# Moving read-outs and tanh behind the next exponentials, and turning the row maxima on VectorE

## The chip, the core and the metric

The kernel runs on one NeuronCore of a Trainium2 chip. Five engines work side by side, each through its own queue in order: TensorE (PE) multiplies matrices into PSUM banks, VectorE (DVE) and ScalarE (ACT) read those banks, GpSimd (POOL) works on SBUF only, and SyncE (SP) issues the transfers. PSUM has eight banks of 128 partitions by 512 fp32 values. The metric is the device time of one execution in microseconds; lower is better.

## The reference

One transformer layer with attention and MLP in parallel, all in fp32, with S = 2048 tokens, D = 512, H = 32 heads of 16, and F = 1792:

```
xn  = layernorm(x)
q, k, v = split(xn @ wqkv)                       # 32 heads of 16
p   = softmax(q k^T / 4)                         # per head, 2048 x 2048
out = x + (p v) @ wo + gelu_tanh(xn @ w1 + b1) @ w2 + b2
```

## The kernel before

**Precision.** Most fp32 matrices are split into a high and a low fp16 part and multiplied by three products (high·high, high·low, low·high). p·v is done in fp32.

**Attention.** Heads are taken in 8 groups of four (NG), query tokens in four blocks of 512 (NQB), keys in 16 blocks of 128. A pair (group, query block) is called t; there are 32. One *unit* u is a sixteenth of a t, so there are 512 units, and each unit has two *halves* (a = 0, 1). The softmax needs the maximum of each query row before the exponentials, so there are two passes over the scores, both on PE, the second one 19 units (LEAD) behind the first:

- `s_half` (L245): scores with queries on the partitions, into a bank of the list S; VectorE reduces the tile to row maxima, tile `mt` (L257). 4 tiles a unit.
- `s_end` (L260): at the last unit of a t, `mneg` takes the maximum over the key blocks (L268). The maxima must then lie along the free dimension, as two extra rows (high and low fp16 part) of the query operand `qst`, rows 62 and 63 of each half of 64, where a row of constants in `kst` subtracts them inside the product. A function `store` is left in a dictionary and called in the first half of the next unit (L674). It transposes `mneg` with two fp32 products against the identity into a bank of S (L275), VectorE splits it to `mhl` (L278, L279), two transfers write `m_d` in memory (L282) and four read it back into `qst` (L287).
- `e_half` (L291): scores with keys on the partitions, into a bank of the list T; ScalarE takes exp into `pe` (L302). 4 tiles a unit; the first that needs the maxima of t is in unit 16t + 19.
- `v_half` (L305): p·v, accumulated over a whole t in the bank of the list V. At the end ScalarE copies it to `osb` (L328), and VectorE, POOL and transfers divide it by the row sums.

**Dense work.** All other products (projections of q and k, MLP, output projection) are cut into *groups* that fill one bank: 12 products for a hidden tile (56 of them, 14 per block of 512 tokens), 42 for an output tile (16). PE is used as two halves of 64 rows: in each half-unit one side does p·v and the other side `dense` (L575) adds three or four products of the current group (`pace`), each cut in four tiles of 32 columns by `tiled` (L195; the products themselves are issued on L169). When a group is complete, `ended` calls `end` (L444), which emits the read-out on ScalarE and returns the group's bank. The read-outs are: `hh` (L1045, hidden tiles), `yt` (L1068, MLP output tiles), `pf` (L502, projections of q and k), `ys` (L1109, output projection).

**gelu.** After `hh`, POOL makes three steps (L1025 to L1027), ScalarE the tanh on tile `t1` (L1014, shown as `t`), POOL four more steps (L1019 to L1022) that end in the two fp16 parts `g`. These steps are put off by units: `later(n, fn)` runs fn n units later at the unit's end (`tick`, L233), and `pooled` gives POOL about 2.5 us of steps a unit.

**Order.** From unit 16 on the order is written out by hand: `unit` (L633) emits, for each half, two score tiles and two exponential tiles (the *burst*: S, E, S, E), then p·v and dense products, then what is due. Each engine keeps that order. The projections of the first key group run before, in a set-up stage ordered by a planner.

**Banks.** `free_banks` (L102) holds lists. S has three banks; the bank for p·v comes from V the first time and then from S, to which it returns. T has three; the group's bank comes from D the first time, and from the front of T afterwards, since `hold("D", "T")` gives a bank that returns to the end of T. So four banks serve the exponential tiles and the group: while a group holds one, three rotate; in the moment between two groups, T holds four. `banks` takes from the front of the list and puts it back at the end at once: waiting for the earlier reader is left to the hardware semaphores.

```
def end(self):
    self.finish(self.bank)
    if self.key is not None:
        free_banks[self.key[1]].append(self.key[0])
```

Of the kernel before, what the change touches and what calls it, by code (L numbers as in the profile page):

```python
# [8 lines left out]
F32 = mybir.dt.float32  # L9
F16 = mybir.dt.float16  # L10
I32 = mybir.dt.int32
AF = mybir.ActivationFunctionType
ALU = mybir.AluOpType
AX = mybir.AxisListType
# [3 lines left out]
P = 128  # L18
S = 2048
# [8 lines left out]
NQB = S // QB  # L28
NG = H // 4
# [13 lines left out]
MROW = 1024.0  # L43
# [4 lines left out]
def layer_kernel(ctx: ExitStack, tc: tile.TileContext, x, wqkv, wo, w1, b1, w2, b2, out):  # L48
    nc = tc.nc
    x = x.flatten_outer_dims()  # L50
    out = out.flatten_outer_dims()

    def pool(stack, name, bufs=1, space=None, side=None):
        kw = {k: v for k, v in (("space", space), ("side", side)) if v is not None}
        return stack.enter_context(tc.tile_pool(name=name, bufs=bufs, **kw))

    const = pool(ctx, "const")
    work = pool(ctx, "work")
    ps = pool(ctx, "ps", space=PSUM)
    dram = pool(ctx, "dram", space=DRAM)  # L60
# [4 lines left out]
    w1_d = dram.tile([NF // 2, P, 2, 2, NC, P], F16, name="w1_d")  # L65
    w2_d = dram.tile([P, 2, NF, D], F16, name="w2_d")
    acc_d = dram.tile([S, D], F32, name="acc_d")
    m_d = dram.tile([NG * NQB, 16, 2, P], F16, name="m_d")
    ot_d = dram.tile([D, 2, S], F16, name="ot_d")
    den_d = dram.tile([NG * NQB, 2, 4, QB], F32, name="den_d")  # L70

# [1 line left out]
    ident = const.tile([P, P], F32, name="ident")  # L73
# [19 lines left out]
    nc.gpsimd.memset(vv[:, :, H * VW:], 0.0)  # L93
    wo_s = const.tile([P, 2, NC, D], F16, name="wo_s")
    sexp = const.tile([P, 4], F32, name="sexp")

    mnegs = [const.tile([P, 32], F32, name=f"mneg{i}") for i in range(2)]
    for m in mnegs:
        nc.gpsimd.memset(m, 0.0)


    free_banks = {"S": [0, 1, 2], "T": [3, 4, 5], "D": [6], "V": [7]}  # L102
# [1 line left out]
    def bank_tile(k, tag):  # L104
        return ps.tile([P, QB], F32, tag=f"B{k}", bufs=1, name="p" + tag)

    def banks(tag):
        k = free_banks[tag].pop(0)
        free_banks[tag].append(k)
        return bank_tile(k, tag)  # L110
# [48 lines left out]
    def given(engine, ns):  # L159
        backlog[engine] += ns  # L160
# [26 lines left out]
    def enter():  # L187

        if left:
            goal[0] = f"turn{counted[0]}"  # L190
            for p in left:
                tc.add_to_no_dep_group(goal[0], p.ins)
            left.clear()
# [9 lines left out]
    def fetch_scale(m):  # L203

        scale_of[m] = nc.scalar.alloc_register(f"sexp{m}")
        nc.scalar.reg_load(scale_of[m], sexp[0:1, m:m + 1].bitcast(I32))

    mt_of, ptiles, pv_of, stores = {}, {}, {}, {}
    queue, slot = [], [0]

    def later(n, fn, local=False):
        queue.append((slot[0] + n, fn, local))

    def run_due():
        due = sorted((q for q in queue if q[0] <= slot[0]), key=lambda q: q[0])
        queue[:] = [q for q in queue if q[0] > slot[0]]
        for q in due:
            q[1]()


    steps, room = [], [0]
# [4 lines left out]
    def run_steps(all_of_them=False):  # L226
        room[0] = min(room[0], 0) + POOL_NS
        while steps and (room[0] > 0 or all_of_them):
            ns, fn = steps.pop(0)
            room[0] -= ns  # L230
            fn()
# [5 lines left out]

    def flush():

        while steps or any(q[2] for q in queue):  # L240
            run_due()
            run_steps(True)
            slot[0] += 1

# [15 lines left out]
    def s_end(u):  # L260

        t, i = divmod(u, 16)
        if i < 15:
            return
        g, qb = divmod(t, NQB)
        qs = qst[g % 2]
        mneg = mnegs[t % 2]
        nc.vector.tensor_reduce(mneg[:, :16], mt_of[t].rearrange("p h t k -> p (h t) k"), axis=AX.X, op=ALU.max, negate=True)  # L268
        given("dve", 220)

        def store():

            pt = banks("S")
            for a in range(2):
                nc.tensor.matmul(pt[32 * a:32 * a + 32, :64], mneg[64 * a:64 * a + 64, :],  # L275
                                 ident[64 * a:64 * a + 64, 64 * a:64 * a + 64], start=True, stop=True)
            mhl = work.tile([64, 2, 64], F16, name="mhl", bufs=2)
            nc.vector.tensor_scalar_mul(mhl[:, 0], pt[:64, :64], 1.0 / MROW)  # L278
            nc.vector.scalar_tensor_tensor(mhl[:, 1], pt[:64, :64], 1.0 / MROW, mhl[:, 0], op0=ALU.mult, op1=ALU.subtract)  # L279
            given("dve", 300)  # L280
            for a in range(2):
                nc.sync.dma_start(m_d[t, :, :, 64 * a:64 * a + 64], mhl[32 * a:32 * a + 16])  # L282
            for p in range(2):
                for a in range(2):
                    h = 2 * p + a
                    dst = qs[p][qb][64 * a + 62:64 * a + 64, :].rearrange("r (t q) -> r t q", q=P)
                    nc.sync.dma_start(dst, m_d[t, 4 * h:4 * h + 4].rearrange("t r q -> r t q"))  # L287

        stores[t] = store

    def e_half(u, n):  # L291

# [264 lines left out]
                cur[0], spent[0] = None, True  # L557
        return cur[0]

    def ended():  # L560

        if cur[0] is not None and cur[0].over():
            done, cur[0] = cur[0], None
            done.end()

    def burst(gen, n):

# [49 lines left out]

    def land():

        while extra[0] is not None:  # L620
            for side in range(2):
                if extra[0] is not None:
                    spare(None, side)
        if cur[0] is not None:
            enter()
        for side in range(2):
            while cur[0] is not None and cur[0].left(side):
                nc.tensor.drain()
                while cur[0].left(side):
                    cur[0].product(side)  # L630
        ended()

    def unit(gen):  # L633


        u = pos[0]
        e = u - LEAD
        if e >= 0 and e % (2 * NQB * 16) == 0 and e < NU:
            fetch_scale(e // (2 * NQB * 16))
        if u == LEAD and cur[0] is not None:  # L640
            burst(gen, cur[0].left())
        pos[0] += 1
        for a in range(2):
            for b in range(2 * a, 2 * a + 2):
                if u < NU:
                    s_half(u, b)
                elif u > NU:
                    spare(gen, b % 2)
                if 0 <= e < NU:
                    e_half(e, b ^ 1)  # L650
            if u < LEAD:
                burst(gen, LFILL[u - 16] // 2)
            if e >= 0:
                enter()

                w, r = (e - 2, 1) if a == 0 else (e - 1, 0)
                live = 0 <= w < NU
                new = r == 0 and w % 16 == 0
                if live and not new:
                    v_half(w, r)  # L660
                dense(gen, 1 - r)
                if live and new:
                    v_half(w, r)

                for user, goes_on in (("V", live and not (r == 1 and w % 16 == 15)),
                                      ("D", cur[0] is not None and not cur[0].over())):
                    leave(user, goes_on)
                for k in backlog:
                    backlog[k] = max(0, backlog[k] - HALF)
                if live and r == 1:  # L670
                    v_end(w)
                ended()

            if a == 0 and u % 16 == 0 and u // 16 - 1 in stores:  # L674
                stores.pop(u // 16 - 1)()
        if u < NU:
            s_end(u)
        tick()
# [325 lines left out]
    def mlp():  # L1004
# [3 lines left out]
        done = set()  # L1008

        def gelu(hh, g, b, f):  # L1010
            t1 = m2.tile([P, QB], F32, name="t1", bufs=2)

            def tanh():
                nc.scalar.activation(t1, t1, AF.Tanh, scale=GELU_C * GELU_A)  # L1014
                given("act", 600)
                later(1, rest, True)

            def rest():
                pooled((690, lambda: nc.gpsimd.tensor_scalar(t1, t1, 1.0, gs[:, 1:2], op0=ALU.add, op1=ALU.mult)),  # L1019
                       (1280, lambda: nc.gpsimd.tensor_tensor(t1, t1, hh, op=ALU.mult)),  # L1020
                       (620, lambda: nc.gpsimd.tensor_scalar(g[:, 0, f, :], t1, 1.0, 0.0, op0=ALU.mult, op1=ALU.add)),
                       (1160, lambda: nc.gpsimd.tensor_tensor(g[:, 1, f, :], t1, g[:, 0, f, :], op=ALU.subtract)),  # L1022
                       (0, lambda: done.add((b, f))))

            pooled((1040, lambda: nc.gpsimd.tensor_tensor(t1, hh, hh, op=ALU.mult)),  # L1025
                   (620, lambda: nc.gpsimd.tensor_scalar(t1, t1, 1.0, 1.0 / GELU_A, op0=ALU.mult, op1=ALU.add)),
                   (1280, lambda: nc.gpsimd.tensor_tensor(t1, t1, hh, op=ALU.mult)),  # L1027
                   (0, lambda: later(2, tanh, True)))

        for b in range(NQB):  # L1030
            xb = xbs[b]
# [19 lines left out]
            for q in range(4):  # L1051
                t = b * 4 + q
# [13 lines left out]
                def store(yp, xa=xa, t=t):  # L1066
# [9 lines left out]
                            lambda n, b=b: (b, n // 3) in done, pace=SLOW if b < 2 else MEAN)  # L1076
# [151 lines left out]
```

## Time and profile before

| | |
|---|---|
| runs shown | 1526.5, 1520.38 and 1525.09 us, median 1525.09 |
| profiled execution | 1520.55 us, its span 1518.8 us |
| busy share of the span | PE 98%, VectorE 92%, ScalarE 82%, POOL 44% |
| granted clock of PE | 0.996 on average |
| score reductions (L257) | 2048, 1304.5 us busy together |
| exponentials (L302) | 2048, 1100.8 us busy together |

The page is one execution: its first part gives the busy time of each engine, its second the span in 40 slices, its fourth the chain of work that ended last, its fifth the costliest groups of instructions with the idle time ahead of them and what ended it. Two matrix products on different row halves or column tiles overlap, so a busy PE does not say how much of it works. A row of the timeline gives start, length, engine, line, output and input, and in brackets the idle time before it and who ended that.

The score passes start at about 38 us; the hand-written order runs from about 107 us to the end. Projections of q and k fill the dense side until about 304 us, then come hidden stage and output stage for each of the four blocks (to 1385 us), then the output projection.

### The profile page before, as it was taken

Reading aid. Unit: us, or ns where it says so; the run is one execution under the profiler, and the core shown is the slowest. Engines: PE = TensorE matmul, PEld = TensorE weight load, DVE = VectorE, ACT = ScalarE, POOL = GpSimd, SP = SyncE. Lnnn points to the kernel's source line nnn. Section 1 sums busy time; section 2 is a strip of 40 time slices with the busy share of each in tenths; the row PEclk is TensorE's granted clock in tenths of the full one; section 3 lists DMA queues with packets and bytes.
Section 4 is the critical chain, followed back from the end, with each engine's and each line's share of the span. In section 5 each row is a group of like instructions: output and inputs, shape, how many; then the busy total and the mean of one; then the engine's idle time right before and its main releaser. Section 6 shows DMA issues by size and latency. Waiting matters only on the chain.

```text
span 1518.8 us, 86848 instructions
## 1 busy us (share of the span) xinstructions
PE 1489.5 (98%) x39407; PEld 815.9 (54%) x39407; DVE 1402.2 (92%) x2367; ACT 1245.6 (82%) x2318; POOL 664.5 (44%) x686
## 2 busy tenths in 40 slices
PE   8999999999999999999999999999999999999998
PEld 3434555555555555555555555555555555555553
DVE  7899989999999999999999999999999999999933
ACT  5327778899988888898888898988888898888884
POOL 4113597547771112777411167751116775211110
PEclk9999999999999999999999999999999999999998
DMA  6454567542122201121011211122101201121422
GB/s 208 127 155 158 166 219 211 180 126 77 58 69 66 61 26 42 36 84 50 23 49 41 66 42 40 36 78 63 34 25 56 77 27 29 50 60 50 136 65 95
DMA packets 113674, 123.76 MB, mean 81 GB/s; under 512 B 24988, under 2 KB 85276, under 8 KB 113304
## 3 DMA queue, kind: packets, MB, share of 16 engines
q1 hardware_dynamic: 113304, 118.21, 25.4%
q8 instruction: 308, 5.05, 1.4%
q14 instruction: 62, 0.51, 0.1%
HBM read 80.61 MB, written 37.34 MB: 78 GB/s over the span
## 4 chain that ended last, share of the span: by engine, by line
PE 79%; DVE 16%; issue 2%; ACT 2%; DMA 1%; POOL 0%; SPq 0%; POOLq 0%
PE pV L169 23%; PE pD L169 19%; PE pT L169 17%; PE pS L169 16%; DVE mt L257 13%; PE pT L435 1%; PE pD L435 1%; DVE amx L709 1%; ACT pe L302 1%; ACT t L1014 1%; PE pT L528 1%; PE pV L528 0%; DMA m_d<-mhl 0%; DMA xs<-in_A_x_dram 0%; DMA wch<-in_B_w_dram 0%
## 5 line engine op out<-in xcount | busy, mean ns | idle before, releaser
L257 DVE TENSOR_REDUCE mt<-pS 128x1 f32<-128x512 f32 x2048 | 1304.5, 684 | 52.5 <-PE pS L169 34.8
L302 ACT ACTIVATE pe<-pT 128x512 f32<-128x512 f32 x2048 | 1100.8, 599 | 162.9 <-PE pS L169 78.6
L169 PE MATMUL pV<-pe,vv 64*32 64x512 f32 x8192 | 1076.3, 595 | 0.1
L169 PE MATMUL pT<-qst,kst 64*32 64x512 f16 x8192 | 718.3, 378 | 8.8 <-ACT pe L302 7.9
L169 PE MATMUL pS<-kst,qst 62*32 62x512 f16 x8192 | 624.3, 378 | 5.2 <-DVE mt L257 3.6
L169 PEld LDWEIGHTS <-kst 64*32 64x32 f16 x8192 | 285.7, 91 | 203.9 <-issue 103.6
L169 PEld LDWEIGHTS <-qst 62*32 62x32 f16 x8192 | 273.3, 92 | 206.3 <-issue 58.2
L169 PE MATMUL pD<-w_s,g 64*32 64x512 f16 x5376 | 364.6, 376 | 0.0
L169 PE MATMUL pD<-xb,wc 64*32 64x512 f16 x5376 | 360.9, 377 | 0.0
L169 PEld LDWEIGHTS pV<-pe,vv 64*32 64x32 f32 x8192 | 181.0, 105 | 88.3 <-PE pV L169 4.3
L1070 POOL TENSOR_TENSOR xa<-xa,yt 128x512 f32<-128x512 f32 x16 | 20.5, 1282 | 319.0 <-ACT yt L1068 319.0
L169 PEld LDWEIGHTS <-wc 64*32 64x32 f16 x5376 | 116.9, 91 | 41.6
L169 PEld LDWEIGHTS <-g 64*32 64x32 f16 x5376 | 112.2, 91 | 45.3
L169 PE MATMUL pD<-xt,wqk_h 64*32 64x512 f16 x2016 | 134.7, 377 | 1.7 <-issue 1.5
L1025 POOL TENSOR_TENSOR t<-hh 128x512 f32<-128x512 f32 x56 | 58.3, 1041 | 132.7 <-ACT hh L1045 121.8
L358 POOL TENSOR_TENSOR osb<-osb,rb 128x512 f32<-128x512 f32 x31 | 39.9, 1287 | 135.1 <-DMA rb<-den_d 76.0
L1027 POOL TENSOR_TENSOR t<-t,hh 128x512 f32<-128x512 f32 x56 | 71.9, 1284 | 4.7
L1020 POOL TENSOR_TENSOR t<-t,hh 128x512 f32<-128x512 f32 x56 | 71.8, 1281 | 4.7
L1022 POOL TENSOR_TENSOR g<-t,g 128x512 f16<-128x512 f32 x56 | 65.2, 1165 | 4.7
L169 PEld LDWEIGHTS <-wqk_h 64*32 64x32 f16 x2016 | 47.5, 92 | 23.4 <-issue 6.2
L169 PE MATMUL pD<-wo_s,oc 64*32 64x512 f16 x828 | 54.5, 378 | 0.0
L1045 ACT ACTIVATE hh<-pD,b_s,fac 128x512 f32<-128x512 f32 x56 | 43.6, 779 | 9.4 <-PE pT L169 3.3
(141 smaller groups left out, 862.4 us busy)
## 6 DMA issues: line engine op xcount, KB each, us to landing
wch<-in_B_w_dram SPq DMA_DIRECT2D x28, 512.0 KB
wc<-w_d SPq DMA_DIRECT2D x56, 256.0 KB
qk_d<-stg SPq DMA_DIRECT2D x32, 256.0 KB
rb<-den_d SPq DMA_DIRECT2D x124, 64.0 KB
w_d<-wsp SPq DMA_DIRECT2D x28, 256.0 KB
kst<-qk_d SPq DMA_DIRECT2D x128, 48.0 KB
qst<-qk_d SPq DMA_DIRECT2D x128, 48.0 KB
xs<-in_A_x_dram SPq DMA_DIRECT2D x16, 256.0 KB
```

The costliest lines, as they stand in the source:

```text
L169: p = nc.tensor.matmul(*args, **kw)
L257: nc.vector.reduce_max(mt_of[t][:, n, qt, kb:kb + 1], s, axis=AX.X)
L302: nc.scalar.activation(pe, st, AF.Exp, scale=scale_of[g // 2])
L358: pooled((1280, lambda: nc.gpsimd.tensor_tensor(osb, osb, rb, op=ALU.mult)), (620, lambda: nc.gpsimd.tensor_scalar(ot[:, 0], osb, 1.0, 0.0 ...
L435: nc.tensor.matmul(self.bank, lhs, rhs, start=start, stop=self.last and self.over())
L528: nc.tensor.matmul(pj, xt[:, i, c, t * P:(t + 1) * P], wh[j][:, c, :], start=(n == 0), stop=(n == 11))
L1020: (1280, lambda: nc.gpsimd.tensor_tensor(t1, t1, hh, op=ALU.mult)),
L1022: (1160, lambda: nc.gpsimd.tensor_tensor(g[:, 1, f, :], t1, g[:, 0, f, :], op=ALU.subtract)),
L1025: pooled((1040, lambda: nc.gpsimd.tensor_tensor(t1, hh, hh, op=ALU.mult)), (620, lambda: nc.gpsimd.tensor_scalar(t1, t1, 1.0, 1.0 / GELU_A ...
L1027: (1280, lambda: nc.gpsimd.tensor_tensor(t1, t1, hh, op=ALU.mult)),
L1045: nc.scalar.activation(hh, hp, AF.Identity, scale=scale, bias=bias)
L1070: add = lambda: nc.gpsimd.tensor_tensor(xa, xa, yt, op=ALU.add)
```

## The change

Two things are moved and one is replaced.

- **Read-outs.** `ended` can now leave the group's `end` in a list `ends`; `unit` calls `ended(False)`, and `one_more()` takes one entry in the next half, after that half's burst and before its p·v and dense products. So the read-out stands on ScalarE behind the two exponentials of the next burst instead of ahead of them, and the bank returns to T after that burst has drawn its two banks. The next group still starts in the same half as before.
- **tanh.** When it is due, it goes to a list `extras`, of which `one_more` takes one entry when no read-out is waiting. So it too stands behind a burst's exponentials, and never directly next to a read-out.
- **Maxima.** `s_end` no longer leaves a function for the next unit. VectorE splits `mneg` into high and low part side by side (`mh`, 128 x 32 fp16) and turns it with its 32x32 transposition into `mc`, in which partition 32b + c holds column c of the 32 queries of block b. Four transfers write that to `m_d` (32 rows of 64 bytes each, before two of 128-byte runs), and four read it back in rows of 1024 bytes (before 256). The two products on PE, their bank of S, the two constant tiles `mnegs` and their clearing are gone. All this is emitted at the end of the last unit of t, half a unit and a burst earlier than before.

```
-    m_d = dram.tile([NG * NQB, 16, 2, P], F16, name="m_d")
+    m_d = dram.tile([NG * NQB, 2, 16, P], F16, name="m_d")
...
     def flush():
-        while steps or any(q[2] for q in queue):
+        settle()
+        while steps or extras or any(q[2] for q in queue):
             run_due()
+            while extras:
+                extras.pop(0)()
             run_steps(True)
...
-        mneg = mnegs[t % 2]
-        nc.vector.tensor_reduce(mneg[:, :16], mt_of[t].rearrange("p h t k -> p (h t) k"), axis=AX.X, op=ALU.max, negate=True)
+        mneg = work.tile([P, 16], F32, name="mneg", bufs=2)
+        nc.vector.tensor_reduce(mneg, mt_of[t].rearrange("p h t k -> p (h t) k"), axis=AX.X, op=ALU.max, negate=True)
         given("dve", 220)

-        def store():
+        mh, mc = (work.tile([P, 32], F16, name=x, bufs=2) for x in ("mh", "mc"))
+        nc.vector.tensor_scalar_mul(mh[:, :16], mneg, 1.0 / MROW)
+        nc.vector.scalar_tensor_tensor(mh[:, 16:], mneg, 1.0 / MROW, mh[:, :16], op0=ALU.mult, op1=ALU.subtract)
+        nc.vector.transpose(mc, mh)
+        rows = m_d[t].rearrange("j c q -> (j c) q")
+        for b in range(4):
+            nc.sync.dma_start(rows[:, 32 * b:32 * b + 32], mc[32 * b:32 * b + 32])
+        for p in range(2):
             for a in range(2):
-                nc.tensor.matmul(pt[32 * a:32 * a + 32, :64], mneg[64 * a:64 * a + 64, :],
-                                 ident[64 * a:64 * a + 64, 64 * a:64 * a + 64], start=True, stop=True)
...
+                h = 2 * p + a
+                nc.sync.dma_start(qs[p][qb][64 * a + 62:64 * a + 64, :],
+                                  m_d[t, :, 4 * h:4 * h + 4].rearrange("j t q -> j (t q)"))
...
+    ends, extras = [], []
+
+    def ended(at_once=True):
         if cur[0] is not None and cur[0].over():
             done, cur[0] = cur[0], None
-            done.end()
+            ends.append(done.end)
+            if at_once:
+                settle()
+
+    def settle():
+        while ends:
+            ends.pop(0)()
+
+    def one_more():
+        if ends:
+            ends.pop(0)()
+        elif extras:
+            extras.pop(0)()
...
             if e >= 0:
+                one_more()
                 enter()
...
-                ended()
-
-            if a == 0 and u % 16 == 0 and u // 16 - 1 in stores:
-                stores.pop(u // 16 - 1)()
+                ended(False)
...
-                   (0, lambda: later(2, tanh, True)))
+                   (0, lambda: later(2, lambda: extras.append(tanh), True)))
```

More of the change, by code (lines that the diff above doesn't have):

```diff
@@ L95, in layer_kernel @@
     sexp = const.tile([P, 4], F32, name="sexp")
-    mnegs = [const.tile([P, 32], F32, name=f"mneg{i}") for i in range(2)]
-    for m in mnegs:
-        nc.gpsimd.memset(m, 0.0)
     free_banks = {"S": [0, 1, 2], "T": [3, 4, 5], "D": [6], "V": [7]}
@@ L206, in fetch_scale @@
         nc.scalar.reg_load(scale_of[m], sexp[0:1, m:m + 1].bitcast(I32))
-    mt_of, ptiles, pv_of, stores = {}, {}, {}, {}
+    mt_of, ptiles, pv_of = {}, {}, {}
     queue, slot = [], [0]
@@ L266, in s_end @@
         qs = qst[g % 2]
-        mneg = mnegs[t % 2]
-        nc.vector.tensor_reduce(mneg[:, :16], mt_of[t].rearrange("p h t k -> p (h t) k"), axis=AX.X, op=ALU.max, negate=True)
+        mneg = work.tile([P, 16], F32, name="mneg", bufs=2)
+        nc.vector.tensor_reduce(mneg, mt_of[t].rearrange("p h t k -> p (h t) k"), axis=AX.X, op=ALU.max, negate=True)
         given("dve", 220)
-        def store():
-            pt = banks("S")
-            for a in range(2):
-                nc.tensor.matmul(pt[32 * a:32 * a + 32, :64], mneg[64 * a:64 * a + 64, :],
-                                 ident[64 * a:64 * a + 64, 64 * a:64 * a + 64], start=True, stop=True)
[L277 to L289, printed above, removed]
+        mh, mc = (work.tile([P, 32], F16, name=x, bufs=2) for x in ("mh", "mc"))
[6 more added lines that the diff above has]
+        for p in range(2):
+            for a in range(2):
+                h = 2 * p + a
+                nc.sync.dma_start(qs[p][qb][64 * a + 62:64 * a + 64, :],
+                                  m_d[t, :, 4 * h:4 * h + 4].rearrange("j t q -> j (t q)"))
     def e_half(u, n):
@@ L558, in group @@
         return cur[0]
-    def ended():
+    ends, extras = [], []
+    def ended(at_once=True):
         if cur[0] is not None and cur[0].over():
             done, cur[0] = cur[0], None
-            done.end()
+            ends.append(done.end)
[9 more added lines that the diff above has]
+            extras.pop(0)()
     def burst(gen, n):
@@ L618, in land @@
     def land():
+        settle()
         while extra[0] is not None:
```

## The prediction

> **What bounds the kernel now.** I read the page first, for the engines' shares and the chain that ended last; then the busy table by stage, restricted to the score reductions of line 257; then the order in time around single events.
>
> ```profile
> span 1518.8 us, 86848 instructions
> PE 1489.5 (98%) x39407; PEld 815.9 (54%) x39407; DVE 1402.2 (92%) x2367; ACT 1245.6 (82%) x2318; POOL 664.5 (44%) x686
> ...
> DMA  6454567542122201121011211122101201121422
> ...
> PE 79%; DVE 16%; issue 2%; ACT 2%; DMA 1%; POOL 0%; SPq 0%; POOLq 0%
> ```
>
> The DMA line is its busy share in 40 slices, in tenths. PE carries four fifths of the chain, VectorE most of the rest, ScalarE 2%. A unit is four reductions and four exponentials, so the count of reductions in a window, divided by four, gives the pace. The eight windows below are in turn the hidden-layer stage and the output stage of each of the four token blocks; columns: window, length, VectorE busy (instructions), clock, DMA share, GB/s.
>
> ```profile
> 306.20:440.00 133.80, 125.01 (x197) 1.00 0.28 84
> 440.00:585.50 145.50, 141.48 (x225) 1.00 0.17 48
> 585.50:719.50 134.00, 125.13 (x197) 1.00 0.20 59
> 719.50:865.40 145.90, 141.74 (x225) 1.00 0.14 42
> 865.40:998.60 133.20, 125.07 (x197) 1.00 0.15 45
> 998.60:1124.90 126.30, 122.67 (x192) 1.00 0.17 49
> 1124.90:1258.80 133.90, 125.03 (x197) 1.00 0.18 53
> 1258.80:1385.20 126.40, 122.55 (x193) 1.00 0.14 40
> ```
>
> One edge reduction aside, a hidden window is 49 units: 534.9 us over 196, 2.729 us a unit. The last two output windows are 48 units each and carry the same dense load (3.5 products a half on average): 252.7 us over 96, 2.632. So the hidden stages pay 0.097 us a unit, 19.0 us in all, for what the output stages have less of: read-outs of 56 groups and 56 tanh. Where that goes is seen in time, ScalarE first and then PE:
>
> ```profile
> 929.74 2.28 ACT L302 ACTIVATE pe<-pT 128x512 f32<-128x512 f32 x4 [0.28 <-PE pS L169]
> 932.15 0.78 ACT L1045 ACTIVATE hh<-pD,b_s,fac 128x512 f32<-128x512 f32 x1
> 932.83 0.62 ACT L1014 ACTIVATE t<-t 128x512 f32<-128x512 f32 x1
> 933.35 2.05 ACT L302 ACTIVATE pe<-pT 128x512 f32<-128x512 f32 x4
> 933.99 0.40 PE L169 MATMUL pT<-qst,kst 64*32 64x512 f16 x4 [0.39 <-ACT pe L302]
> ```
>
> The read-out and the tanh stand ahead of the next burst's exponentials; these begin at 933.35, 1.1 us late, and the score product that wants their bank begins at 933.99. A lone read-out costs less, as in an output stage:
>
> ```profile
> 826.47 2.27 ACT L302 ACTIVATE pe<-pT 128x512 f32<-128x512 f32 x4 [0.28 <-PE pS L169]
> 828.82 0.69 ACT L1068 ACTIVATE yt<-pD,gs 128x512 f32<-128x512 f32 x1
> 829.40 2.05 ACT L302 ACTIVATE pe<-pT 128x512 f32<-128x512 f32 x4
> 831.69 2.29 ACT L302 ACTIVATE pe<-pT 128x512 f32<-128x512 f32 x4 [0.24 <-PE pS L169]
> ```
>
> Two units from 826.47 to 831.69 are 5.22 us. An undisturbed unit is 2.55 (847.03 to 849.58 below), so the yt cost 0.12.
>
> **The change, part 1: read-outs and tanh behind the exponentials.** The order of PE's products stays; only ScalarE's order and the PSUM banks change. It gives back the 19.0 us of the hidden stages and the price of the other read-outs:
>
> ```profile
> L1045 ACT ACTIVATE hh<-pD,b_s,fac 128x512 f32<-128x512 f32 x56 | 43.6, 779 | 9.4 <-PE pT L169 3.3 <-PE pS L169 2.8
> L502 ACT ACTIVATE pf<-pD 128x512 f32<-128x512 f32 x22 | 13.1, 597 | 7.4 <-PE pD L435 2.9 <-PE pS L169 2.3 <-PE pT L169 2.2
> L1068 ACT ACTIVATE yt<-pD,gs 128x512 f32<-128x512 f32 x16 | 11.0, 688 | 1.5 <-PE pT L169 0.2
> L1109 ACT ACTIVATE ys<-pD,gs 128x512 f32<-128x512 f32 x8 | 5.5, 687 | 1.0 <-PE pT L169 0.6
> ```
>
> That is 22 + 16 + 8 = 46 others; at 0.12 for yt and somewhat less for the shorter pf I take 0.10, 4.6 us. The gain if nothing takes their place: 23.6 us.
>
> Something does. The group's bank used to return to the rotation at the end of its half, before the next burst drew its two banks; now it returns after they are drawn. Follow the list of free T banks. Before, it held four at that moment, and every score tile got a bank whose last exponential was three tiles back. After, it holds three; the burst takes z and x, the read-out returns k behind them, the new group takes y from the front, and the second burst again gets z and x: two tiles back. k comes only in the third. So in each of these 102 places the second score tile of a burst waits for the second exponential of the burst just before. Undisturbed, these stand so:
>
> ```profile
> 847.03 2.28 ACT L302 ACTIVATE pe<-pT 128x512 f32<-128x512 f32 x4 [0.28 <-PE pS L169]
> 847.52 0.59 ACT L302 ACTIVATE pe<-pT 128x512 f32<-128x512 f32 x1
> 847.75 0.57 PE L169 MATMUL pT<-qst,kst 64*32 64x512 f16 x5
> 849.58 1.79 ACT L302 ACTIVATE pe<-pT 128x512 f32<-128x512 f32 x3 [0.28 <-PE pS L169]
> ```
>
> The second exponential ends at 848.11. The last product of the next burst's second tile is the one that ends at 848.32; a product takes 0.38, so it starts at 847.94. It would have to wait until 848.11 plus the signal's way (at 933.99 the product came about 0.05 after the exponential that began at 933.35 and takes 0.59): 0.22 us. V stands behind it in PE's queue, so the wait is paid in full where PE is full; with four dense products a half the tile comes a little later anyway. Between 0 and 0.22 I take 0.20: 102 x 0.20 = 20.4 us lost. Net of part 1: -3.2 us.
>
> The Trainium skill, Perfetto Trace Analysis, Optimization Strategy, says that the same gap repeating for a stretch on the engine that should be saturated can mean too little PSUM for the next tile. By that rule the kernel still lacks a bank, and moving the read-out only moves the gap; the row at 933.99 agrees, since there PE waits for a bank.
>
> The later hh and tanh (one to one and a half units each) I cost at nothing. PE's dense products stand in the same halves in both built programs, and an output group takes the hidden tiles in order, three products each, so the last of 14 is wanted after 39 products at three or four a unit: about ten units, 26 us, after the stage's end. POOL's seven steps and the tanh are 7 us by the costs in the code, plus some four units of waiting slots, now five or six. If that cover went, PE would wait for POOL at four places, once a block.
>
> **Part 2: the maxima.** VectorE and the one PE wait at such a boundary, before:
>
> ```profile
> 809.84 0.68 DVE L257 TENSOR_REDUCE mt<-pS 128x1 f32<-128x512 f32 x1
> 810.55 0.22 DVE L268 TENSOR_REDUCE mneg<-mt 128x16 f32<-128x64 f32 x1
> 810.69 1.28 DVE L257 TENSOR_REDUCE mt<-pS 128x1 f32<-128x512 f32 x2
> 811.89 0.21 DVE L278 TENSOR_SCALAR mhl<-pS 64x64 f16<-64x64 f32 x1
> 812.13 0.22 DVE L279 SCALAR_TENSOR_TENSOR mhl<-pS,mhl 64x64 f16<-64x64 f32 x1
> 812.02 0.40 PE L169 MATMUL pS<-kst,qst 62*32 62x512 f16 x4 [0.16 <-DVE mt L257]
> ```
>
> Removed: the PE products of line 275 and the S bank they drew, and the two mhl instructions between reductions. Added: three in a row behind mneg (split high, split low, transposition). Nearest rows:
>
> ```profile
> L758 DVE SCALAR_TENSOR_TENSOR sd<-sd 128x4 f32<-128x4 f32 x4 | 0.6, 158 | 0.1
> L346 DVE RECIPROCAL dn<-dn 64x32 f32<-64x32 f32 x31 | 10.4, 334 | 0.0
> ```
>
> I take 0.17 for each split (16 columns, where the row has four) and, with no row for a transposition, 0.20, nearer the first row (bounds 0.16 from it and 0.33 from the second, 32 columns and a slow operation). With 0.03 between dependent instructions (809.84 + 0.68 to 810.55) the stretch from 810.52 is 0.9, less 0.08 by which a reduction overlaps its predecessor: 0.82. The next reduction then ends at 810.52 + 0.82 + 0.68 = 812.02, and the second score tile of that half, which now needs this reduction's bank (the S rotation is one shorter), comes at 812.07 against 812.02 today. Today's came after the later reduction because line 275 had drawn a bank. So one wait replaces the other at about equal price; VectorE, left 0.2 further behind, makes PE wait about 0.1 once more. I take +0.10 for 29 boundaries under full load, +2.9 us (bounds -5 and +9).
>
> The Trainium skill, VectorE: DVE Perf Modes, Rules for kernel authors, advises fewer operations in a chain, not cheaper links; the same page's The three transpose paths gives 311 ns for 128x128. At 0.31 for the transposition part 2 would cost an estimated 6 us.
>
> The way through memory grows from six transfers to eight:
>
> ```profile
> 812.37 1.22 SPq L282 DMA_DIRECT2D m_d<-mhl  x2
> 814.82 1.16 SPq L287 DMA_DIRECT2D qst<-m_d  x4
> 818.05 0.39 PE L169 MATMUL pT<-qst,kst 64*32 64x512 f16 x4
> ```
>
> Four stores at 0.61 from 811.4 end at 813.8; with the same 1.23 between them and the loads, and 0.29 a load, the last is issued by 816.2, against 815.98 now, and the first product that reads them stands at 818.05. In SP's queue the stores now stand ahead of the transfers of the unit's end instead of behind them; these wait for the transposition too and follow the loads. They are fetches for later units. I count 0.
>
> **Sum.** -3.2 + 2.9 + 0 = -0.3 us on the profiled execution's 1520.55 (span 1518.8), which is 4.5 below the median of the runs shown, 1525.09. On the median: about 1524, no change.
>
> **The rivals.** (A) The two-tile reuse is absorbed, because exponentials ahead of read-outs run earlier than in my undisturbed unit. For it: the margin is 0.2 us and PE starts tiles of its two row halves out of step. Against it: 847.52 is already undisturbed. At 0 us each: -23.6 + 2.9, 1504; it counts as faster below 0.13 us each. (B) Slower: the exponential waited for is itself late, after a tanh or an osb copy. At 0.36 us each, 36.7 - 23.6 + 2.9 = +16, 1541; it decides above 0.27. Against it: in the built program mostly eight exponentials, two units, lie between a tanh and the next read-out, enough for ScalarE to catch up. (C) The loads land late in the first third, where the DMA share of the page is highest; at 0.8 us for 31 boundaries, +25, 1550. Against it: about 1.8 us in the rows above.
>
> **How the numbers follow.** Forecast 0.43, A 0.30, B 0.17, C 0.10. 0.5% is 7.6 us, about what a measurement of this kernel can tell from no change. A gives nearly all of faster (0.30), B and C of slower (0.28), the forecast of same (0.42). The range, 1507 to 1541, cuts off the ends of A and of B, and C; the forecast's own is 1517 to 1532.
>
> **What would show it.** Right: ScalarE has hh and t behind two exponentials and the hidden windows fall below 2.70 us a unit; the output windows rise by about 0.02; PE's wait "pT <- ACT pe" keeps or grows its count; the four short VectorE instructions stand in one stretch of 0.8 us. Wrong: hidden windows at 2.63 with output windows unchanged (A); a growing wait for qst<-m_d (C); a transposition well off 0.2 us.

## The result and the profile after

The changed kernel takes 1532.67 us (median of 6 runs, 1529.49 to 1535.42) against 1523.78 for the kernel before (6 runs): ratio 1.0061, 95% interval 1.0041 to 1.0082. It is slower by about 9 us, just over what a measurement can tell from no change. The forecast was no change at 1524, the range 1507 to 1541. The profiled execution of the changed kernel took 1533.31 us.

The page of the changed kernel, its first part and its chain of work (by engine, then by line):

```profile
span 1531.4 us, 86595 instructions
...
PE 1486.2 (97%) x39279; PEld 812.7 (53%) x39279; DVE 1418.9 (93%) x2400; ACT 1245.4 (81%) x2317; POOL 663.5 (43%) x683
...
PE 75%; DVE 19%; issue 2%; SPq 2%; DMA 1%; ACT 1%; POOL 0%; ACTq 0%; POOLq 0%
PE pV L165 22%; PE pD L165 18%; PE pT L165 16%; PE pS L165 16%; DVE mt L256 14%; SPq L393 1%; DVE mh L271 1%; PE pT L427 1%; PE pD L427 1%; DVE mh L272 1%; DVE amx L716 1%; DMA wch<-in_B_w_dram 1%; PE pT L520 1%; PE pV L520 0%; DVE mneg L267 0%
```

PE's share of the chain fell from 79% to 75% and VectorE's rose from 16% to 19%. Two of the new instructions, the splits on L271 and L272, stand in the chain with 1% each, although there are only 32 of each and they have 16 columns.

The eight stages again, the hidden-layer and the output stage of each token block in turn, by the score reductions (L256 now); columns: window, length, VectorE busy (instructions), clock, DMA share, GB/s:

```profile
312.11:444.02 131.91, 124.26 (x197) 1.00 0.31 91
444.02:591.22 147.20, 140.64 (x225) 1.00 0.16 44
591.22:723.09 131.87, 123.75 (x196) 1.00 0.21 59
723.09:871.06 147.97, 140.55 (x224) 1.00 0.15 41
871.06:1004.86 133.80, 124.85 (x197) 1.00 0.16 45
1004.86:1132.53 127.67, 121.30 (x192) 1.00 0.17 48
1132.53:1267.62 135.09, 124.49 (x197) 0.99 0.19 53
1267.62:1396.36 128.74, 122.39 (x193) 1.00 0.14 40
```

The hidden windows are 532.7 us together, 2.2 less than before; the output windows are 551.6 against 544.1. Every window holds about three boundaries between two t, so both parts of the change are mixed in each. I therefore take the two apart by the starts of the reductions: the *pair* is the last unit of a t and the unit after it, from first reduction to first reduction; the hidden stages are summed without the units of such pairs.

| | hidden stages without the pairs, us | mean pair, t = 2 to 30, us |
|---|---|---|
| before | 466.2 | 5.673 |
| after | 456.0 | 6.282 |

The hidden stages gained 10.2 us and 29 pairs lost 29 x 0.609 = 17.7. That is +7.5 of the 12.6 us between the two spans. Of the rest 1.2 us lie behind the last reduction and 2.5 in the projections of q and k, where the profiles of all kernels below but the one that returns the bank early differ by up to 6 us without order (171.4 to 177.1 without their pairs); the profiled execution of before was also 3.2 below its median here, that of the changed kernel 0.6 above.

**Where a pair loses.** VectorE at a boundary where both splits are held up, then POOL and PE beside it (start, length, engine, line, operation, tiles):

```profile
556.52 1.29 DVE L256 TENSOR_REDUCE mt<-pS 128x1 f32<-128x512 f32 x2
557.85 0.22 DVE L267 TENSOR_REDUCE mneg<-mt 128x16 f32<-128x64 f32 x1
558.10 0.80 DVE L271 TENSOR_SCALAR mh<-mneg 128x16 f16<-128x16 f32 x1
558.93 1.19 DVE L272 SCALAR_TENSOR_TENSOR mh<-mneg,mh 128x16 f16<-128x16 f32 x1
560.16 0.21 DVE L273 STREAM_TRANSPOSE mc<-mh 128x32 f16<-128x32 f16 x1
...
557.70 1.17 POOL L352 TENSOR_TENSOR ot<-osb,ot 128x512 f16<-128x512 f32 x1
558.82 1.27 POOL L1071 TENSOR_TENSOR xa<-xa,b_b 128x512 f32<-128x512 f32 x1
...
560.99 0.40 PE L165 MATMUL pS<-kst,qst 62*32 62x512 f16 x4 [1.96 <-DVE mt L256]
```

The first split ends at 558.90, POOL's instruction at 558.87. The second split ends at 560.12, POOL's next at 560.09. Then PE has waited 1.96 us for the next reduction to free a bank of S. At another boundary POOL is idle:

```profile
516.21 0.22 DVE L267 TENSOR_REDUCE mneg<-mt 128x16 f32<-128x64 f32 x1
516.46 0.17 DVE L271 TENSOR_SCALAR mh<-mneg 128x16 f16<-128x16 f32 x1
516.67 0.17 DVE L272 SCALAR_TENSOR_TENSOR mh<-mneg,mh 128x16 f16<-128x16 f32 x1
516.88 0.21 DVE L273 STREAM_TRANSPOSE mc<-mh 128x32 f16<-128x32 f16 x1
```

Over all 32 boundaries (duration in ns: shortest, median, longest):

```profile
L271 DVE TENSOR_SCALAR mh<-mneg x32: 167/183/1175, 108.1 to 1463.7; 128x16 f16<-128x16 f32 x32
...
L272 DVE SCALAR_TENSOR_TENSOR mh<-mneg,mh x32: 167/176/1201, 108.8 to 1463.9; 128x16 f16<-128x16 f32 x32
...
L273 DVE STREAM_TRANSPOSE mc<-mh x32: 204/211/213, 109.5 to 1464.1; 128x32 f16<-128x32 f16 x32
```

Of the 64 splits 22 took over 0.25 us. In all 22 a POOL instruction was running when the split started, and the split ended 0.02 to 0.04 us after that instruction's end. Where POOL's instruction ended within the split's ordinary time, or POOL was only waiting, the split was short. The transposition is never touched. At the 14 boundaries of t = 2 to 30 with two short splits the pair is 5.764 us, at the other 15 it is 6.765.

PE's wait for the reduction over the whole span (total, times, longest), in the kernel before and then in the changed one:

```profile
PE pS L169 <- DVE mt L257: 3.6, 14, 1.4
```

```profile
PE pS L165 <- DVE mt L256: 24.9, 33, 2.0
```

**Where the hidden stages gain.** ScalarE around a read-out in the changed kernel, and three products on PE (the second score tiles of three bursts):

```profile
920.36 1.09 ACT L294 ACTIVATE pe<-pT 128x512 f32<-128x512 f32 x2 [0.28 <-PE pS L165]
921.33 0.78 ACT L1052 ACTIVATE hh<-pD,b_s,fac 128x512 f32<-128x512 f32 x1
922.00 2.27 ACT L294 ACTIVATE pe<-pT 128x512 f32<-128x512 f32 x4
924.15 0.63 ACT L1021 ACTIVATE t<-t 128x512 f32<-128x512 f32 x1
...
920.00 0.39 PE L165 MATMUL pT<-qst,kst 64*32 64x512 f16 x4
921.50 0.40 PE L165 MATMUL pT<-qst,kst 64*32 64x512 f16 x4
922.80 0.42 PE L165 MATMUL pT<-qst,kst 64*32 64x512 f16 x4
```

The read-out stands behind two exponentials, as intended. The second of these ends at 921.45, and the second score tile of the next burst starts 0.05 later, at 921.50: 1.50 us after its predecessor, where a half takes 1.28. That is the wait of 0.22 for the bank two tiles back.

### The profile page after: what moved, and what is told of

It reads as the page before. It is cut to its first block, busy times and chain, and to the rows that moved or that the text cites. A ratio compares the mean times of both kernels' runs of the same rounds, so it can differ in the third digit from the quotient of the medians.

```text
span 1531.4 us, 86595 instructions
## 1 busy us (share of the span) xinstructions
PE 1486.2 (97%) x39279; PEld 812.7 (53%) x39279; DVE 1418.9 (93%) x2400; ACT 1245.4 (81%) x2317; POOL 663.5 (43%) x683
## 4 chain that ended last, share of the span: by engine, by line
PE 75%; DVE 19%; issue 2%; SPq 2%; DMA 1%; ACT 1%; POOL 0%; ACTq 0%; POOLq 0%
PE pV L165 22%; PE pD L165 18%; PE pT L165 16%; PE pS L165 16%; DVE mt L256 14%; SPq L393 1%; DVE mh L271 1%; PE pT L427 1%; PE pD L427 1%; DVE mh L272 1%; DVE amx L716 1%; DMA wch<-in_B_w_dram 1%; PE pT L520 1%; PE pV L520 0%; DVE mneg L267 0%
## 5 line engine op out<-in xcount | busy, mean ns | idle before, releaser
L256 DVE TENSOR_REDUCE mt<-pS 128x1 f32<-128x512 f32 x2048 | 1296.8, 683 | 45.4 <-PE pS L165 22.7
L294 ACT ACTIVATE pe<-pT 128x512 f32<-128x512 f32 x2048 | 1113.9, 598 | 192.3 <-PE pS L165 86.2
L1026 POOL TENSOR_SCALAR t<-t,gs 128x512 f32<-128x512 f32 x56 | 38.9, 695 | 57.8 <-ACT t L1021 57.6
```

Of the source, the lines that this page charges most:

```text
L256: nc.vector.reduce_max(mt_of[t][:, n, qt, kb:kb + 1], s, axis=AX.X)
L294: nc.scalar.activation(pe, st, AF.Exp, scale=scale_of[g // 2])
```

## The experiments

The theory after the result: part 1 gains some microseconds, and part 2 loses more, because a split that reads SBUF can stand still until an instruction of POOL ends. The rivals were that part 1 is the loss, that the chain of four instructions is too long whatever POOL does, and, for part 1, that the late return of the bank eats most of its gain. All ratios are to the kernel before on the same chip (1523.92 us for the first four runs, 1523.45 for the others).

### Part 1 alone

The kernel before with the moved read-outs and tanh; `store` and its products on PE stay.

```
+                one_more()
                 enter()
...
-                ended()
+                ended(False)
...
-                   (0, lambda: later(2, tanh, True)))
+                   (0, lambda: later(2, lambda: extras.append(tanh), True)))
```

> Only the read-outs and the tanh are moved; the maxima go by PE as before. Theory (VectorE's two splits wait for POOL at the boundaries, and part 1 by itself gains): about 7 us faster than before, ratio 0.995 to 0.996, hidden windows near 2.68 us a unit, and the two units around a boundary as long as before, 5.6 us. Rival (the longer boundaries come from read-outs that now stand elsewhere): boundaries of 6.2 us here too, and no gain.

Measured: 1517.32 us, ratio 0.9956 (0.9942 to 0.997). Part 1 is a gain of 6.6 us. Its hidden windows, which hold no split now:

```profile
314.17:446.04 131.87, 125.31 (x196) 1.00 0.32 91
...
591.44:722.05 130.61, 124.51 (x196) 1.00 0.21 60
...
868.14:999.67 131.53, 125.59 (x197) 1.00 0.16 46
...
1125.61:1257.06 131.45, 125.08 (x197) 1.00 0.20 54
```

That is 525.5 us over 196 units, 2.681 a unit, against 2.729. The mean pair is 5.669 us, as before the change (5.673), so the longer boundaries don't come from the moved read-outs.

### Part 2 alone

The changed kernel with read-outs and tanh in their old places.

```
-                one_more()
                 enter()
...
-                ended(False)
+                ended()
...
-                   (0, lambda: later(2, lambda: extras.append(tanh), True)))
+                   (0, lambda: later(2, tanh, True)))
```

> Only the maxima are turned on VectorE; read-outs and tanh stay where they were. Theory: 14 to 18 us slower than before, ratio 1.009 to 1.012, with splits of up to 1.2 us that end with a POOL instruction. Rival (read-outs at the boundary are the cause): within 3 us of before.

Measured: 1542.37 us, ratio 1.0126 (1.0111 to 1.0142). Part 2 is a loss of about 18 us, a little more than expected. Of its 64 splits 21 took over 0.25 us, the longest 1.22, and each of these ended 0.02 to 0.04 us after an instruction of POOL. The pairs are 5.761 us at the 12 boundaries where both splits are short and 6.793 at the other 17, 6.366 on average; the hidden stages without them are 466.9, as before. PE's wait for the reductions is as in the changed kernel:

```profile
PE pS L165 <- DVE mt L256: 24.5, 34, 2.1
```

The two parts add up roughly: -0.44% and +1.26% against +0.61% together.

### The splits read PSUM

The changed kernel with one edit: `mneg` lies in a bank of S and no longer in SBUF. The chain of four instructions, the transfers and POOL's work are the same; a bank of S is drawn, as in the kernel before.

```
-        mneg = work.tile([P, 16], F32, name="mneg", bufs=2)
+        mneg = banks("S")[:, :16]
```

> The changed kernel, with the maxima of a block written to a PSUM bank of list S instead of SBUF, so that neither split reads two operands in SBUF. Theory (a split waits for POOL because it needs both SBUF ports of VectorE): every split takes 0.2 to 0.25 us, boundaries lose 0.5 us, about 14 us faster than the changed kernel, near 1518. Rival (the cost is the length of the chain of four instructions and the S bank): as slow as the changed kernel, 1532, or slower, since a bank of S is taken again.

Measured: 1519.5 us, ratio 0.9977 (0.9967 to 0.9988). The splits, then one boundary at which POOL is at work throughout:

```profile
L271 DVE TENSOR_SCALAR mh<-pS x32: 161/174/176, 109.1 to 1448.1; 128x16 f16<-128x16 f32 x32
...
L272 DVE SCALAR_TENSOR_TENSOR mh<-pS,mh x32: 160/174/175, 109.8 to 1448.3; 128x16 f16<-128x16 f32 x32
```

```profile
638.37 0.18 DVE L271 TENSOR_SCALAR mh<-pS 128x16 f16<-128x16 f32 x1
638.58 0.17 DVE L272 SCALAR_TENSOR_TENSOR mh<-pS,mh 128x16 f16<-128x16 f32 x1
638.78 0.21 DVE L273 STREAM_TRANSPOSE mc<-mh 128x32 f16<-128x32 f16 x1
...
637.67 1.28 POOL L350 TENSOR_TENSOR osb<-osb,rb 128x512 f32<-128x512 f32 x1
```

None of the 64 splits is long, although at 19 of the 32 boundaries a POOL instruction was running when the first split started. The pair falls to 5.877, and PE's wait returns to what it was:

```profile
PE pS L165 <- DVE mt L256: 4.1, 8, 1.6
```

So it is not the length of the chain but where the splits read: 13 us of the changed kernel's time go with the long splits. This is net of the bank of S that is drawn again, which is no gain by itself: the pairs of 5.877 are longer than the 5.764 of the changed kernel's boundaries with two short splits. What stays of part 2 is 0.2 us a pair over part 1 alone, 6 us over 29 pairs; by the medians 2.2 us.

### The bank is returned early

Part 1 alone, but the group's bank returns to T at the end of its half, as before; only the read-out comes later.

```
+        def back(self):
+            if self.key is not None:
+                free_banks[self.key[1]].append(self.key[0])
+                self.key = None
...
-            if at_once:
+            if not at_once:
+                done.back()
+            else:
                 settle()
```

> Part 1 alone, but the group's bank goes back to the list at the end of its half, as before, while the read-out itself stays behind the next burst; so score tiles again reuse a bank three tiles back. Theory (each moved read-out costs a wait of 0.1 to 0.2 us for a bank two tiles back): 10 to 20 us faster than part 1 alone, 1500 to 1508. Rival (that wait is absorbed): the same as part 1 alone, within 3 us.

Measured: 1581.52 us, ratio 1.0395 (1.038 to 1.0409). The expectation was wrong, and the waits of PE say why:

```profile
PE pT L169 <- ACT hh L1071: 42.1, 56, 1.0
PE pT L169 <- ACT yt L1094: 11.5, 16, 0.8
PE pT L169 <- ACT pf L509: 10.2, 20, 0.7
```

The bank that returns early is drawn by the first tile of the second burst, and its read-out now stands behind two exponentials. PE waits 0.75 us for each of the 56 hidden read-outs. The late return, with its 0.22 us, was the cheaper wait.

### The read-out between the two exponentials

Part 1 alone, with the read-out after the first exponential of the burst; the bank returns there.

```
                 if 0 <= e < NU:
                     e_half(e, b ^ 1)
+                if e >= 0 and b == 2 * a and ends:
+                    ends.pop(0)()
+                    fresh[0] = True
...
-                one_more()
+                if not fresh[0]:
+                    one_more()
+                fresh[0] = False
```

> Part 1 alone (maxima as before), but the read-out stands between the two exponentials of the next burst, and the group's bank returns to T there; tanh stays behind both. By the list of T the second burst then gets z and k: z's exponential is the first of the burst before and not the second, and k's read-out ends one exponential earlier. Theory (the late return of the bank costs 0.22 us at some 71 to 102 places): that wait mostly goes, 10 to 17 us less than part 1 alone, 1500 to 1508 us. Rival (the wait only passes to the first tile of the burst, which in part 1 alone has a median margin of 0.10 us to its exponential two tiles back): within 3 us of part 1 alone, 1514 to 1520. Second rival (as in the run that returned the bank early: PE waits for the read-out): over 1530.

Measured: 1525.63 us, ratio 1.0016 (1.0005 to 1.0028). Not 1500 to 1508: 8 us slower than part 1 alone. One place, ScalarE and then the product that draws the read-out's bank:

```profile
934.46 0.60 ACT L305 ACTIVATE pe<-pT 128x512 f32<-128x512 f32 x1 [0.28 <-PE pS L169]
934.95 0.77 ACT L1070 ACTIVATE hh<-pD,b_s,fac 128x512 f32<-128x512 f32 x1
935.61 1.57 ACT L305 ACTIVATE pe<-pT 128x512 f32<-128x512 f32 x3
...
935.77 0.40 PE L169 MATMUL pT<-qst,kst 64*32 64x512 f16 x4
```

The read-out ends at 935.72, the product starts at 935.77; in 53 of the 56 hidden places the second score tile of the next burst starts 0.05 us after the read-out's end, in the other three about 0.1. I had put the read-out's end one exponential earlier; but the read-out takes 0.78 and the exponential it displaces 0.59, so it ends 0.2 us later than that exponential would have. The bank wait went from the exponential to the read-out and grew. This is the second rival's mechanism, at a smaller price than it gave.

### The tanh in the middle too

Part 1 alone, with whatever is due, read-out or tanh, taken after the first exponential of the burst.

```
                 if 0 <= e < NU:
                     e_half(e, b ^ 1)
+                if e >= 0 and b == 2 * a:
+                    one_more()
...
-                one_more()
                 enter()
```

> As mid, but the tanh too stands between the two exponentials. Theory (where a tanh stands matters only through the exponential that PE waits for next; behind the first exponential of a burst or behind the second is the same slip for ScalarE): within 3 us of mid. Rival (tanh delays the second exponential, whose bank is wanted three tiles later): 5 to 10 us slower than mid.

Measured: 1525.12 us, ratio 1.0002 (0.999 to 1.0013), within 3 us of the run above: behind which exponential of a burst a tanh stands makes no difference that was measured.

### Only the tanh, only the read-outs

Part 1 alone, less one of its two moves each.

```
-                ended(False)
+                ended()
```

> Of part 1 only the tanh is moved: read-outs end their half as before, so no bank comes back late. My theory put the hidden stages' 19.0 us on read-out and tanh together standing ahead of the exponentials. If the two share the cost by their number and the next group's bank stays in time, the move of the tanh alone gains 5 to 9 us: 1515 to 1519. Rival (read-outs alone carry it): 1522 to 1526.

```
-                   (0, lambda: later(2, lambda: extras.append(tanh), True)))
+                   (0, lambda: later(2, tanh, True)))
```

> Of part 1 only the read-outs are moved; the tanh stays at the unit's end, ahead of the next burst. Theory: gains what part 1 gains less what the tanh gives, 1517 to 1524, with the 0.22 us wait for the bank in its place as in part 1 alone. Rival (all of part 1's gain is the read-outs'): 1515 to 1519. Second rival (a tanh ahead of a burst with a read-out behind it delays the awaited exponential, and the wait for the bank grows): 1526 to 1535.

Measured: the tanh alone 1516.09 us, ratio 0.9953 (0.9937 to 0.9968); the read-outs alone 1514.68, ratio 0.9941 (0.9925 to 0.9958). The first is in its expected range; the second is 0.3 us below the nearest of its ranges, that of the rival by which all of part 1's gain is the read-outs'. Each alone gains as much as both together, 6.6 us; the three intervals overlap. The gains don't add, and what they share can be seen at the place of a hidden read-out. There the mean time from the second score tile of one burst to that of the next exceeds the 1.28 us of a half by

| before | tanh only | read-outs only | both | between the exponentials |
|---|---|---|---|---|
| 0.43 us | 0.27 | 0.24 | 0.24 | 0.41 |

In the kernel before, the two tiles of the second burst behind the read-out both wait. The first takes the read-out's own bank: at 49 of the 56 places it starts 0.05 us after the read-out's end. The second takes the bank of the first exponential that stands behind the read-out: at 54 places it starts 0.05 us after that exponential's end. At the place that the prediction shows, the first starts at 932.98, after the read-out that ends at 932.93:

```profile
932.98 0.40 PE L169 MATMUL pT<-qst,kst 64*32 64x512 f16 x4
933.99 0.40 PE L169 MATMUL pT<-qst,kst 64*32 64x512 f16 x4 [0.39 <-ACT pe L302]
```

This place is one of 18 where a tanh stands directly behind the read-out and holds that exponential back further. There the excess is 0.76 us on average; at the other 38 it is 0.27. Moving the tanh takes the long wait away at these 18 and leaves the rest as it is. Moving the read-out takes both away, but puts the 0.22 for the older bank in their place: with the read-outs alone moved, 53 of the 56 places have the second score tile of the next burst 0.05 us behind the exponential two tiles back. The hidden stages without the pairs are 459.8 us with the tanh alone, 457.3 with the read-outs alone, 458.0 with both.

The version with only the read-outs moved has the lowest time of all that ran; it is faster than both kernels (0.4% to 0.8% under the kernel before), and not told apart from part 1 alone.

## Why the prediction was wrong

**Part 1, the forecast of -3.2 us: right in mechanism, a little short in size.** The two-tile reuse was counted at 102 places and the wait priced at 0.22, taken as 0.20. In part 1 alone, of the 71 such places in the MLP stages 93% have the second score tile 0.05 us behind the exponential's end, and there the unit has a median of 2.796 us against 2.576 elsewhere: 0.22. Rival A (absorbed, 1504) is out by that, and so is rival B (0.36). For the hidden stages the prediction's terms make -19.0 + 56 x 0.20 = -7.8; part 1 alone measured -8.2. For the 46 other read-outs they make +4.6. This term isn't settled: the projections of q and k, where 22 of them stand, rose by 4.1 us in the profile of part 1 alone and fell by 1.3 in that of the read-outs alone, and the output stages rose by 0.4 and 1.0. In total part 1 measured -6.6 with bounds -4.6 and -8.8.

The rule cited from the Trainium skill, Perfetto Trace Analysis, Optimization Strategy (the same gap repeating can mean too little PSUM), is borne out: four orders of read-out and bank return gave four different waits for a T bank (0.22 us for the exponential two tiles back in the changed kernel, 0.75 for the read-out with the early return, for the read-out with it between the exponentials, and for the read-out and the exponential behind it in the kernel before), and none was without one. What the prediction drew from it, that the move only moves the gap, falls short: the half at a hidden read-out also became 0.2 us shorter.

**Part 2, the forecast of +2.9 us: this step failed.** The failing term is "I take 0.17 for each split". 0.17 is what a split takes when POOL is quiet; the 32 first splits took 13.5 us together and the 32 second ones 12.0, 0.42 and 0.375 each. The sum of the excess over t = 2 to 30 is 13.8 us, and over the 29 pairs a pair grows by 1.09 us for each microsecond of it. The splits had no bounds of their own, and the part's bounds, -5 and +9, didn't hold the loss of 18, because I looked for rows of the same size and not for rows in the same company. The rest of the step held: the transposition measured 0.211 against 0.20; the stretch from first split to the end of the transposition with POOL quiet is 0.63, with `mneg` 0.89, where the prediction's terms make 0.60 and 0.85; and those pairs cost 5.764 - 5.673 = 0.09 us more than before, where +0.10 was forecast. With splits that don't wait the sum would have been right within a few microseconds: the run whose splits read PSUM is at 1519.5. That 1532.67 lies inside the range of 1507 to 1541 is luck: the upper end is rival B's, late exponentials, and the time was lost elsewhere.

A row of the trace of before could have shown it. VectorE, and POOL beside it:

```profile
151.80 2.03 DVE L959 TENSOR_TENSOR gs<-gs,fac 128x1 f32<-128x1 f32 x1
...
151.68 2.14 POOL L939 TENSOR_TENSOR wsp<-wch,wsp 128x1024 f16<-128x1024 f32 x1
```

A multiplication of one column with two SBUF inputs took 2.03 us and ended, at 153.83, with POOL's instruction. The row quoted for the price (L758, four columns, 158 ns on average) had only four executions, all in the set-up.

The Trainium skill, SBUF — State Buffer, SBUF: two separate sides, states the rule: VectorE and GpSimd share a second pair of SBUF ports as an exclusive lock, held for a whole instruction; a VectorE instruction needs it when it has two SBUF inputs (against a GpSimd instruction that reads SBUF) or runs in a mode with two ports, and the one that comes second blocks fully. This case's traces agree: 22 long splits of 22, lasting up to 1.20 us, end within 0.04 us of the end of POOL's instruction, and with the PSUM operand none of 64 is long. The second split has two SBUF inputs. The first has one, so by the rule it must run in a mode with two ports; its waits fit that, but no run here shows the mode itself. By that rule an estimate from rows of before could have been made: POOL's 686 instructions of 664.5 us last 0.97 us on average, so a split that comes at any moment meets one with a chance of 0.44 and waits for half of it, 0.21 us; 58 splits at 29 boundaries make 12 us, and 13.8 were measured.

**The other steps.** The memory way at 0: right, PE shows no wait for a load of `qst` from `m_d` in the changed kernel, so rival C is out. The delayed hh and tanh at 0: right, no wait of PE for `g` appears. The list of what would show it: the hidden windows are below 2.70 us in part 1 alone (2.681), but 2.718 in the changed kernel, where splits stand in them. The output windows were to rise by 0.02 a unit; in part 1 alone the last two are 252.98 against 252.7, which is no rise. PE's wait "pT <- ACT pe" was to keep or grow its count; it fell from 20 times, 7.9 us, to once, 1.1 us. That was a bad sign to choose: this view counts PE's idle time, and during most of the 0.22 us products on the other row half still run, so the wait is seen in the distances between tiles.

## What to carry to other kernels

Before pricing a small VectorE instruction by its size, look at which memory its operands lie in and what POOL executes at that moment: with SBUF operands in and out it can stand still until POOL's instruction ends, as the two splits did, and a chain of two such instructions can pay twice. Here an operand in PSUM took that away with a one-line edit. When a bank rotation has no spare, moving a late reader chooses for whom the next tile waits and how long, 0.22 to 0.75 us here, and not whether it waits: write the list of banks out for each order, with the durations of both readers, before claiming a gain, and do not add the gains of two moves that shorten the same wait.

## What the hardware showed that was not expected

A split of 128 x 16 took 174 ns at the median from PSUM, and from SBUF 167 to 178 ns where POOL didn't hold it up: the source made no difference there. Not every VectorE instruction between SBUF tiles was held up. In the changed kernel the 32x32 transposition of 128 x 32 fp16 took 204 to 213 ns though POOL was running at 8 of its 32 starts, the reduction to `mneg`, with one input, 211 to 222 ns with POOL running at 17 of 32, and the reciprocal that the prediction quotes, also with one input, no more than 336 ns with POOL running at 14 of 31. Of the chain only the two splits were held up. The second split could be held up by a POOL instruction that started about 0.1 us before it, while the first split was ending, so that one boundary paid 0.80 and then 1.19 us.
